# The third expert's rows turned before the second expert's joins, their twelve sums on GpSimd, and its weight sums issued in two parts around a pair's scatters

## The chip, the cores and the metric

The kernel runs on one core of a Trainium2 chip. TensorE (PE) multiplies matrices, VectorE (DVE) and ScalarE (ACT) do elementwise work and read the results out of PSUM, GpSimd (POOL) does elementwise work on SBUF and issues the scatters, and SyncE (SP) issues the loads. Each engine works through its own queue in the order in which the program was written, and waits where an instruction needs something that another engine or a transfer has not finished. The metric is the device time of one execution in microseconds, as the median of several runs.

## The reference, cut to what matters

A linear attention with a per-channel decay makes 3072 rows of 384 numbers. Each row then goes to one of eight experts, chosen by its largest logit, and back to its own place:

```python
logits = x @ w_gate
expert_idx = np.argmax(logits, axis=1)
...
x_sorted = x[perm]
...
h = np.maximum(x_sorted[lo:hi] @ w1[e], 0.0)
y_sorted[lo:hi] = h @ w2[e]
...
y = y_sorted[inv_perm]
return (gate_w[:, None] * y).astype(np.float32)
```

`w1[e]` is 384 x 1024 and `w2[e]` is 1024 x 384. The change lies in this second half.

## The kernel before, in words

The first half of the program is the attention. It scatters each finished row into a table `xs` in device memory, sorted by expert, with a region for each expert. The second half takes the experts one by one, here counted from 0 as in the code. An expert has up to three tiles of 128 rows (`t` = 0, 1, 2). For experts 0 and 1 the first tile is done early, inside the attention, so these two have two tiles left. What does not fit in three tiles goes to "quads" of small pieces.

One expert passes through these steps:

- `load_expert` (line 500) reads its rows from `xs` into `xrow`, with four loads, and their row numbers and gates into `tg`. `load_pads` (line 515) has to write padding behind the expert's rows first. `load_first_weights` and `load_second_weights` load `w1t` and `w2t`. All of them stand in SP's queue.
- `turn` (line 385) transposes the rows on VectorE (`xT`), and casts the row numbers to `dst`, on ScalarE where it is called from `tasks`.
- The product with `w1` of experts 1 to 7 uses a scheme of 20 block products instead of 24, which needs sums of blocks of the weights (`WEIGHT_SUMS`, 16 steps and 17 instructions, since one step takes two; `prepare_weights`, on GpSimd) and twelve sums of blocks of the rows (`ROW_SUMS`; `sum_rows`, on VectorE, or on GpSimd where a task says `add`).
- `widen_sums` (line 1330) runs the 20 products through five PSUM banks (`hps`), in the order of `WIDE_STEPS`. ScalarE copies some results out (`keep`), VectorE joins results with `join`, which reads PSUM, and `more`, which reads SBUF only, and ScalarE applies the relu (`rect`). The first seven copies come before the first join, and the first join comes after the eighth product. The first result of the ninth weight step, `a11`, is read by the tenth product.
- A third tile goes through `narrow_late`. The first two tiles go through `narrow_pair` (line 1403), the product with `w2`, again with sums: in it VectorE joins two halves of each finished tile in `ysb` (line 1434), and GpSimd scatters the tile to the output (line 253). `ysb` has three buffers, used in turn.

`wide_part` and `pair_part` string these together. The table `TASKS` says which work on other experts' rows stands between the steps of expert `e`: hook 0 at the start of `wide_part`, hook 1 after it, hook 2 inside the pair and hook 3 behind it. A task acts on expert `e + 1`, or on `e + 2` with `>` in front. The order of the work is therefore written out by hand, and each engine's queue follows from it.

The early tiles leave with `narrow_early`, whose two scatters carry no group, so the second waits until the first has landed. The other scatters to the output are in the group "out" and don't wait for each other.

For expert 2 the row sums lie in `rooms[1]`, a buffer of the quads' weights that is free by then (the trace calls it `qw`), and expert 1's hidden values lie in `rooms[2]`, also `qw` in the trace.

Of the kernel before, what the change touches and what calls it, by code (L numbers as in the profile page):

```python
# [62 lines left out]


TASKS = {
    0: ("turn sum12", "", "", ">sum2"),
    1: ("", "turn add6", "sum2", "sum2"),
    2: ("turn", "quad0 sum1", "sum7", "sum4"),
    3: ("turn", "sum6", "sum6", ""),
    4: ("sq00 sq01", "turn sum2", "sum7", "sum3"),  # L70
    5: ("sq02 quad1", "sq03 turn", "sum9", "sum3"),
# [10 lines left out]
PLAIN = (0,)  # L82


GT, AHEAD = 2, 5
WEIGHT_SUMS = """
    as0=a30-a32 a32=a12+a32 as1=a32-a30 as2=a30+a31 as3=a10+a11 as4=as3-a01 a31=a21+a31
    a30=-a30-a31 a11=a01-a11 a11=as1-a11 as5=a02+a22 as6=a20-as5 as7=a00-as4 as5=a30-as5
# [74 lines left out]
def _bc(ap, axis, n):  # L163
    shape = list(ap.shape)
    shape.insert(axis, n)
    return ap[tuple([slice(None)] * axis + [None])].to_broadcast(shape)
# [3 lines left out]
def kernel(  # L170
# [15 lines left out]
    nc = tc.nc  # L186
# [40 lines left out]
    def load_gate():  # L227
# [12 lines left out]
        out=ident,  # L240
# [113 lines left out]
    def load_rows(row, count=C):  # L354

        rows = xs[ds(row, count)] if not isinstance(row, int) else xs[row : row + count]
        n, whole = -(-count // C), count // C
        wholes = rowp.tile([128, TILES * C // BK, DB], F32, name="xrow")
        x = wholes[:, 0 : count // BK]
        tg = rowp.tile([128, TILES, USED - TOK], F32, name="tg", bufs=4)[:, 0:n]  # L360
        reads = load_blocks(x, rows)
        reads.append(
            nc.sync.dma_start(
                tg[:, 0:whole], rows[0 : whole * C, TOK:USED].rearrange("(t p) r -> p t r", p=C)
            ).ins
        )
        if n > whole:
            nc.sync.dma_start(tg[0 : count - whole * C, whole], rows[whole * C :, TOK:USED])
        return {"n": n, "rows": count, "x": x, "tg": tg, "reads": reads, "whole": wholes}
# [61 lines left out]
    def narrow(x, t, w, yp, group="out", order=range(NF), late=None):  # L431
        for f in order:
            nc.tensor.matmul(
                yp,
                lhsT=x["hT"][:, f, t * C : t * C + C],
                rhs=w[1][:, f, :],
                start=f == order[0],
                stop=f == order[-1],
            )
        put(x, t, yp, group, late)  # L440

    def put(x, t, yp, group, late=None):
        ysb = ep.tile([128, DM], F32, name="ysb", bufs=3)
        if x.get("wide") or late is not None:
            nc.scalar.mul(ysb, yp, x["tg"][:, t, 1:2])
        else:
            nc.vector.tensor_scalar(ysb, yp, x["tg"][:, t, 1:2], None, op0=OP.mult)
        leave = lambda: scatter(out, x["dst"][:, t : t + 1], ysb, N - 1, group)
        if late is None:
            leave()  # L450
        else:
            late.append(leave)
# [21 lines left out]
    weights = {}  # L474
# [10 lines left out]
    def load_first_weights(e):  # L485
        w1t = wpool.tile([128, KD, F], F32, name="w1t")
        nc.sync.dma_start(w1t, moe_w1[e].rearrange(W1, p=128))
        weights[e] = [w1t]

    def load_second_weights(e):  # L490
        w2t = wpool.tile([128, NF, DM], F32, name="w2t")
        nc.sync.dma_start(w2t, moe_w2[e].rearrange(W2, p=128))
        weights[e].append(w2t)

    def slot(k, s, most):
        return nc.values_load(
            sloti[0:1, k, s : s + 1], [mybir.EngineType.SP], min_val=0, max_val=most
        )

    def load_expert(e):  # L500

        t = int(e < EARLY)
        x = load_rows(first[e] + t * C, int(FIXED[e]) - t * C)
        if e in RIDE:
            rows = xs[ds(slot(0, RIDE[e], NONE), T)]
            nc.sync.dma_start(x["tg"][C - T :, TILES - 1], rows[:, TOK:USED])
        return x
# [7 lines left out]
    def load_pads(e):  # L515

        end = nc.values_load(
            endi[0:1, e : e + 1],
            [mybir.EngineType.SP],
            min_val=first[e],  # L520
            max_val=first[e] + N,
        )
        ins = nc.sync.dma_start(
            xs[ds(end, TILES * C)].rearrange("(t p) r -> p t r", p=C), _bc(pad, 1, TILES)
        ).ins
        tc.declare_no_dep(ins, group="xs", reason="no row is written twice")
        tc.add_to_no_dep_group("xs", ins)
# [31 lines left out]
    with ExitStack() as st:  # L559
# [300 lines left out]
            x["wide"] = False  # L860

        def narrow_early(x, w, yp, late):
            narrow(x, 0, w, yp, None, late=late)

        def settled(n, rt):

# [277 lines left out]
        over = share()  # L1144
        sums()
        rows_of = {}
        for e in range(4):
            load_pads(e)
            if e < 2:
                rows_of[e] = load_expert(e)  # L1150
# [3 lines left out]
        yp = yt[1].rearrange("p h c -> p (h c)")[:, 0:DM]  # L1154
# [18 lines left out]
    with ExitStack() as st:  # L1173
# [94 lines left out]
        def sums_of(table, at, on):  # L1268

            def one(to, a, b, c, d):  # L1270
                summed(on, at(to), (a or "+", at(b)), (c, at(d)))

            return [
                lambda m=m: one(*m)
                for m in re.findall(r"(\w+)=(-?)(\w+)([+-])(\w+)", table)
            ]
# [29 lines left out]

            return at

        def prepare_weights(x, w):
            x["wa"] = weights_at(w)  # L1310
            for step in sums_of(WEIGHT_SUMS, x["wa"], nc.gpsimd):
                step()

        def prepare_rows(x, held=None):
            x["xa"] = rows_at(x, held)
# [4 lines left out]
        def sum_rows(x, count, other=False):  # L1320
            for name, *step in x["todo"][:count]:
                step[other]()
            x["todo"] = x["todo"][count:]
# [177 lines left out]
        def tasks(e, hook):  # L1501
            for ahead, what, n in re.findall(r"(>?)([a-z]+)(\d*)", TASKS[e][hook]):
                if what in ("turn", "sum", "add"):
                    to = rows_of[e + 1 + len(ahead)]
                    if what == "turn":
                        turn(to, by="scalar")
                        prepare_rows(to, rooms[1] if to is rows_of.get(2) else None)
                    else:
                        sum_rows(to, int(n), what == "add")
                elif what == "quad":  # L1510
                    turn(quads[int(n)], qp)
                else:
                    q, g = int(n[0]), int(n[1])
                    turn_quad(quads[q], slice(g, g + 1))
# [6 lines left out]
        def load_first(e):  # L1521
            if e < E:
                rows_of[e] = load_expert(e)
                load_first_weights(e)
# [26 lines left out]
        for leave in waits:  # L1551
            leave()
        s0 = hidden_sums(rows_of[0], nc.gpsimd)
        load_first(2)
        load_pads(4)
        load_pads(5)
        wide_part(1)
        tasks(1, 1)
        prepare_weights(rows_of[2], weights[2])
        load_first(3)  # L1560
        load_pads(6)
        load_pads(7)
# [1 line left out]
        pair_part(  # L1564
            0, s0, lambda: held.append(hidden_sums(rows_of[1], s1=rooms[2][:, 0:HB, 2 * C :]))
        )
        load_second_weights(2)
        fetch(4)
        pair_part(1, held[0])
# [3 lines left out]
        for e in range(2, E):  # L1573
            x, w = rows_of[e], weights[e]
# [24 lines left out]
    with tc.If(todo > 0):  # L1599
# [80 lines left out]
        with ExitStack() as st:  # L1680
            bank, narrow_late, psz = tile_pools(st)
            hp = st.enter_context(tc.tile_pool(name="hp", bufs=1))
            with tc.For_i(0, E) as e:
# [10 lines left out]
                with tc.For_i(e * REGION + skip, rows_to, C) as at:  # L1694
                    x = load_rows(at)
# [57 lines left out]
```

## Time and profile before

| | us |
|---|---|
| median of 3 runs (lowest to highest) | 379.94 (379.58 to 380.77) |
| the profiled execution's own time | 376.19 |
| its span, first to last instruction | 374.3 |
| TensorE busy | 356.7 (95%) |
| VectorE busy | 280.4 (75%) |
| GpSimd busy | 244.8 (65%) |
| ScalarE busy | 172.1 (46%) |
| mean DMA rate | 253 GB/s |

Times inside the trace count from the first instruction. The attention lasts to about 140 us, expert 0's widening (with the plain scheme) from 140 to 151, expert 1's from 151 to 160, the two pairs of these experts from 160 to 179, expert 2's widening from 179 to 203, and the rest of the experts follow at about 30 us each. A timeline row gives start, length, engine, line, operation and operands, then in brackets the idle time of the engine just before it and what ended it. Neighbouring instructions of one kind are merged, with their number as "x4". A TensorE row counts two matmuls for each one of the program. A wait for several things is put down to the one that came last.

### The profile page before, as it was taken

To read this page: it belongs to the slowest core of one execution; us is meant where nothing else is said; L and a number is where in the kernel's file an instruction comes from. 1 tells how busy PE (TensorE), PEld (TensorE's weight loads), DVE (VectorE), ACT (ScalarE), POOL (GpSimd) and SP (SyncE) were. 2 spreads that over 40 slices of the span, in tenths; PEclk is the share of its full clock that TensorE was granted. 3 is DMA by queue.
4 is the path that set the end of the run, shared out by engine and by line. 5 is a ranking of instruction groups with operands and counts; after the bars stand their busy time and mean duration, and the time that the engine had idled before them with its cause. 6 is when DMAs were issued, how large, how long until landed. Compare 5 with 4: busy or idle time off the path is not lost.

```text
span 374.3 us, 9303 instructions
## 1 busy us (share of the span) xinstructions
PE 356.7 (95%) x3470; PEld 310.2 (83%) x3470; DVE 280.4 (75%) x570; ACT 172.1 (46%) x359; POOL 244.8 (65%) x267
## 2 busy tenths in 40 slices
PE   8999999999999999999829999999999999999993
PEld 8889898988989958989728979879699499499692
DVE  6999989897975875398058956967897985878850
ACT  7999785876443202531314335235335235325410
POOL 6344356748964696349869989859939939947103
PEclk9999999999999999999958999999999999999999
DMA  7999765768994437999954369973799989991051
GB/s 253 395 379 381 250 243 200 256 176 285 391 395 158 176 109 220 273 308 339 387 193 101 133 227 389 245 247 102 239 303 367 284 306 381 373 364 48 12 183 66
DMA packets 56773, 94.86 MB, mean 253 GB/s; under 512 B 20952, under 2 KB 40859, under 8 KB 55696
## 3 DMA queue, kind: packets, MB, share of 16 engines
q1 hardware_dynamic: 53552, 84.55, 68.2%
q0 software_dynamic: 3168, 9.64, 6.8%
q8 instruction: 29, 0.48, 0.5%
q14 instruction: 24, 0.20, 0.2%
HBM read 79.16 MB, written 15.21 MB: 252 GB/s over the span
## 4 chain that ended last, share of the span: by engine, by line
PE 43%; POOL 28%; DMA 12%; issue 10%; SPq 3%; DVE 2%; ACT 1%; POOLq 0%; DVEq 0%; ACTq 0%
PE yps L1416 8%; POOL wsum L1257 7%; POOL was L1266 7%; POOL w1t L1266 6%; PE yps L1238 4%; PE s L683 4%; PE hps L1358 4%; POOL out_dram L253 4%; PE yt L707 4%; PE xp L806 3%; DMA xrow<-xs 3%; DMA xs<-xr,posi 3%; PE s L413 3%; PE hps L413 3%; PE kp L696 2%
## 5 line engine op out<-in xcount | busy, mean ns | idle before, releaser
L253 POOL DMA_INDIRECT out_dram<-ysb,dst x26 | 27.3, 1049 | 55.8 <-DVE ysb L1434 33.9
L1376 ACT ACTIVATE hT<-hT 128x352 f32<-128x352 f32 (+1 forms) x48 | 23.9, 506 | 49.4 <-DVE hT L1346 49.2
L1416 PEld LDWEIGHTS yps<-w2t,hT 128*128 128x128 f32 x224 | 36.4, 190 | 4.5 <-issue 2.5
L649 POOL TENSOR_TENSOR k<-k,r 128x1024 f32<-128x1024 f32 (+1 forms) x11 | 25.1, 2284 | 23.0 <-ACT r L645 17.1
L1416 PE MATMUL yps<-w2t,hT 128*128 128x192 f32 x224 | 39.4, 329 | 0.6 <-ACT held L1430 0.5
L1358 PE MATMUL hps<-xbs,w1t 128*128 128x176 f32 (+2 forms) x216 | 36.0, 310 | 0.1
L253 POOL DMA_INDIRECT xs<-xr,posi x24 | 25.6, 1069 | 13.4 <-issue 4.6
L689 DVE COPY_PREDICATED at<-mpack,s 128x512 f32<-128x512 uint8 x48 | 31.9, 728 | 3.0 <-PE s L683 3.0
L1346 DVE TENSOR_TENSOR hT<-hps,hT 128x352 f32<-128x352 f32 (+1 forms) x42 | 22.2, 528 | 15.4 <-PE hps L1358 9.7
L1358 PEld LDWEIGHTS hps<-xbs,w1t 128*128 128x128 f32 x216 | 32.5, 190 | 0.7 <-issue 0.6
L1369 ACT COPY hT<-hps 128x352 f32<-128x352 f32 (+1 forms) x54 | 24.8, 460 | 17.3 <-PE hps L1358 13.8
L1430 ACT ACTIVATE held<-yps,tg 128x192 f32<-128x192 f32 x32 | 13.0, 421 | 37.9 <-DVE ysb L1434 23.9
L1266 POOL TENSOR_TENSOR was<-w1t 128x256 f32<-128x256 f32 x35 | 29.8, 866 | 0.5
L631 DVE TENSOR_TENSOR_SCAN sum<-g,cap 128x1032 f32<-128x1032 f32 (+1 forms) x14 | 28.1, 2012 | 2.2 <-ACT g L624 2.2
L1434 DVE SCALAR_TENSOR_TENSOR ysb<-yps,tg,held 128x192 f32<-128x192 f32 x32 | 12.5, 413 | 20.1 <-DMA out_dram<-ysb,dst 12.4
L1238 PE MATMUL yps<-qw,hqT 128*32 128x192 f32 (+1 forms) x192 | 26.8, 380 | 0.0
L683 PE MATMUL s<-q,k 64*128 64x128 f32 x384 | 26.3, 281 | 0.2
L1266 POOL TENSOR_TENSOR w1t<-w1t 128x256 f32<-128x256 f32 x28 | 24.9, 889 | 1.6 <-PE yt L1134 1.1
L683 PEld LDWEIGHTS s<-q,k 64*128 64x128 f32 x384 | 22.8, 187 | 2.7 <-issue 0.9
L806 PE MATMUL xp<-wx,ys 128*128 128x104 f32 x192 | 24.9, 279 | 0.2 <-ACT ys L770 0.2
L707 PE MATMUL yt<-at,v 128*48 128x128 f32 x384 | 24.3, 276 | 0.0
L806 PEld LDWEIGHTS xp<-wx,ys 128*128 128x128 f32 x192 | 22.9, 192 | 1.0 <-ACT ys L770 0.3
(191 smaller groups left out, 884.6 us busy)
## 6 DMA issues: line engine op xcount, KB each, us to landing
w1t<-in_moe_w_dram SPq DMA_DIRECT2D x8, 1536.0 KB, 8.9
w2t<-in_moe_w_dram SPq DMA_DIRECT2D x8, 1536.0 KB, 14.1
qw<-in_moe_w_dram SPq DMA_DIRECT2D x16, 768.0 KB, 10.9
qw<-in_moe_w_dram SPq DMA_DIRECT2D x8, 1536.0 KB, 16.3
k<-in_ku_dram SPq DMA_DIRECT2D x12, 512.0 KB, 6.9
q<-in_qu_dram SPq DMA_DIRECT2D x12, 512.0 KB, 6.0
f<-in_fu_dram SPq DMA_DIRECT2D x10, 512.0 KB, 5.8
xs<-pad SPq DMA_DIRECT2D x8, 600.0 KB, 8.2
```

Source lines behind the costliest of these rows:

```text
L253: ins = nc.gpsimd.indirect_dma_start(out=dst, out_offset=bass.IndirectOffsetOnAxis(ap=idx, axis=0), in_=src, in_offset=None, bounds_check= ...
L631: nc.vector.tensor_tensor_scan(x["sum"][:, part].rearrange("p s c -> p (s c)"), x["g"][:, part].rearrange("p s c -> p (s c)"), cap[:, part ...
L649: ins = on.tensor_tensor(k, k, units[u]["r"][:, part], op=OP.mult).ins
L683: done["score"] = nc.tensor.matmul(ps[h][:, p], lhsT=x["k"][r, s], rhs=x["q"][r, s], start=True, stop=True).ins
L689: nc.vector.copy_predicated(x["at"][:, a, h], _bc(causal, 1, HP), x["ps", a][h])
L707: nc.tensor.matmul(x["yt"][a][DP * (h ^ a) : DP * (h ^ a) + D, p], lhsT=x["v"][:, a, 2 * p + h], rhs=x["at"][:, a, h, p], start=p == 0, st ...
L806: nc.tensor.matmul(x["xp", a][:, p], lhsT=x["ys", a][:, p], rhs=wx[:, p, 0:XW] if a else wx[:, p, E:WX], start=True, stop=True,)
L1238: nc.tensor.matmul(yp[r], lhsT=h[:, f, at : at + T], rhs=w[:, f, cols], start=f == order[0], stop=f == order[-1], skip_group_check=True,)
L1257: on.tensor_tensor(to, a, b, op=OP.subtract)
L1266: on.tensor_tensor(to, first[1], second[1], op=op)
L1358: nc.tensor.matmul(banks[n][:, g], lhsT=lhs[:, C * g : C * g + C], rhs=rhs, start=op == "new" and g == 0, stop=True, skip_group_check=True,)
L1416: nc.tensor.matmul(to, lhsT=h[:, f], rhs=w[:, f], start=start and f == 0, stop=f == HB - 1, skip_group_check=True,)
```

## The change

Expert 2's rows are turned at the start of expert 1's `wide_part` and not behind it. All twelve sums of its rows are on GpSimd, where six were before and six were spread over VectorE's queue. Its 17 weight instructions come in two parts: eight steps (nine instructions) ahead of the first pair, and the other eight behind it. The turn of expert 3's rows is written at the end of pair 1 and not at the start of expert 2's widening; its place in VectorE's queue stays. Expert 2's rows are loaded ahead of the pads of expert 3, and the two early scatters join the group "out".

```diff
 TASKS = {
-    0: ("turn sum12", "", "", ">sum2"),
-    1: ("", "turn add6", "sum2", "sum2"),
-    2: ("turn", "quad0 sum1", "sum7", "sum4"),
+    0: ("turn sum12", "", "", ""),
+    1: ("turn add12", "", "", ">turn"),
+    2: ("", "quad0 sum1", "sum7", "sum4"),
...
-GT, AHEAD = 2, 5
+GT, AHEAD, HALFWAY = 2, 5, 8
...
-            narrow(x, 0, w, yp, None, late=late)
+            narrow(x, 0, w, yp, "out", late=late)
...
-        for e in range(4):
+        for e in range(3):
             load_pads(e)
...
-        def prepare_weights(x, w):
+        def prepare_weights(x, w, count=None):
             x["wa"] = weights_at(w)
-            for step in sums_of(WEIGHT_SUMS, x["wa"], nc.gpsimd):
+            x["left"] = sums_of(WEIGHT_SUMS, x["wa"], nc.gpsimd)
+            sum_weights(x, len(x["left"]) if count is None else count)
+
+        def sum_weights(x, count):
+            for step in x["left"][:count]:
                 step()
+            x["left"] = x["left"][count:]
...
         s0 = hidden_sums(rows_of[0], nc.gpsimd)
-        load_first(2)
+        rows_of[2] = load_expert(2)
+        load_pads(3)
+        load_first_weights(2)
         load_pads(4)
         load_pads(5)
         wide_part(1)
-        tasks(1, 1)
-        prepare_weights(rows_of[2], weights[2])
+        prepare_weights(rows_of[2], weights[2], HALFWAY)
...
         pair_part(
             0, s0, lambda: held.append(hidden_sums(rows_of[1], s1=rooms[2][:, 0:HB, 2 * C :]))
         )
+        sum_weights(rows_of[2], len(rows_of[2]["left"]))
```

GpSimd's queue from expert 0's hidden sums (`hT`) to pair 0's scatters, before. The rows `qw<-` are the sums of expert 2's rows, `w1t` and `was` are its weight sums, and the scatters write `out_dram`:

```order
L1257 TENSOR_TENSOR hT<-hT 128x4x128
L1266 TENSOR_TENSOR qw_2121<-xT 128x192 x2
L1266 TENSOR_TENSOR qw_2121<-xT,qw_2121 128x192 x2
L1266 TENSOR_TENSOR qw_2121<-qw_2121,xT 128x192
L1266 TENSOR_TENSOR qw_2121<-xT 128x192
L1266 TENSOR_TENSOR was_2361<-w1t 128x256
...
L1263 TENSOR_TENSOR w1t<-w1t 128x256
L1266 TENSOR_TENSOR w1t<-w1t 128x256
...
L1266 TENSOR_TENSOR w1t<-w1t,was_2379 128x256
L253 DMA out_dram<-ysb,dst 3072x384 x4
```

And after:

```order
L1257 TENSOR_TENSOR hT<-hT 128x4x128
L1266 TENSOR_TENSOR qw_2110<-xT 128x192 x2
L1266 TENSOR_TENSOR qw_2110<-xT,qw_2110 128x192 x2
L1266 TENSOR_TENSOR qw_2110<-qw_2110,xT 128x192
...
L1266 TENSOR_TENSOR qw_2110<-xT,qw_2110 128x192 x4
L1266 TENSOR_TENSOR was_2367<-w1t 128x256
...
L1263 TENSOR_TENSOR w1t<-w1t 128x256
L253 DMA out_dram<-ysb,dst 3072x384 x2
L1266 TENSOR_TENSOR w1t<-w1t 128x256
...
L1266 TENSOR_TENSOR w1t<-w1t,was_2471 128x256
L253 DMA out_dram<-ysb,dst 3072x384 x2
```

The sums of rows are twelve and not six, the weight sums are parted behind L1263, and pair 0's two scatters stand in the gap. Pair 1's two stay behind the second part.

VectorE's queue at expert 1's joins (L1346, `qw_2122` being its hidden values), before, from its last row sum (`xbs`) to the first join, and from the last join to pair 0's sums:

```order
L1266 TENSOR_TENSOR xbs_2163<-xT,xbs_2151 128x128
L1346 TENSOR_TENSOR qw_2122<-hps,qw_2122 128x2x128
...
L1346 TENSOR_TENSOR qw_2122<-qw_2122,hold 128x2x128
L393 STREAM_TRANSPOSE xT<-xrow 128x12x3x32
L1257 TENSOR_TENSOR hT<-hsum,hT 128x4x128
```

And after, where the joins are L1351:

```order
L1266 TENSOR_TENSOR xbs_2152<-xT,xbs_2140 128x128
L393 STREAM_TRANSPOSE xT<-xrow 128x12x3x32
L1351 TENSOR_TENSOR qw_2111<-hps,qw_2111 128x2x128
...
L1351 TENSOR_TENSOR qw_2111<-qw_2111,hold 128x2x128
L1257 TENSOR_TENSOR hT<-hsum,hT 128x4x128
```

The transpose of expert 2's rows moved from behind sixteen joins to ahead of them. Six row sums further down in this queue are gone.

ScalarE's queue at the start of expert 1's widening, before, from expert 0's last relu (L427) on (L1369 copies results out of PSUM):

```order
L427 ACTIVATE hT<-hps 128x2x256 x4
L1369 COPY qw_2122<-hps 128x2x128 x7
L1376 ACTIVATE qw_2122<-qw_2122 128x2x128
L1369 COPY hold<-hps 128x2x128
L1369 COPY qw_2122<-hps 128x2x128
```

And after:

```order
L427 ACTIVATE hT<-hps 128x2x256 x4
L400 CAST dst<-tg 128x3
L1374 COPY qw_2111<-hps 128x2x128 x7
L1381 ACTIVATE qw_2111<-qw_2111 128x2x128
L1374 COPY hold<-hps 128x2x128
```

The cast of expert 2's row numbers, which reads `tg`, stands now ahead of the seven copies. Before it stood behind all of expert 1's relus.

## The prediction

> **What bounds the kernel now.** I read the page's slices first, then busy time in short windows, then each engine's timeline around the place where they break. Experts count from 0 as in the code: the third expert, whose rows are moved, is expert 2, and a "pair" is `narrow_pair` of one expert.
>
> ```profile
> PE   8999999999999999999829999999999999999993
> PEclk9999999999999999999958999999999999999999
> ```
>
> TensorE (PE) is full in nearly every slice. The one dip away from the ends is slices 20 and 21 of 40 (9.36 us each), where the granted clock drops too.
>
> ```profile
> 186.00:188.00 2.00, 0.00 (x0) 0.00 (x0) 0.00 (x0) 0.00 (x0) 1.70 (x2) 1.00 1.05 371
> 188.00:190.00 2.00, 0.00 (x0) 0.00 (x0) 0.00 (x0) 0.00 (x0) 0.14 (x1) 0.56 1.07 381
> ...
> 198.00:200.00 2.00, 2.00 (x12) 2.00 (x12) 1.97 (x4) 0.89 (x2) 1.92 (x3) 0.88 0.36 77
> ```
>
> Columns: length, busy PE, weight load, VectorE (DVE), ScalarE (ACT), GpSimd (POOL), clock, DMA share, GB/s. From 186 to 190 nothing computes except two scatters on GpSimd, and the clock is at 0.56 after 188; it is back at 0.88 only in 198 to 200.
>
> ```profile
> 178.85 0.81 PE L1358 MATMUL hps<-xT,was 128*128 128x192 f32 x4
> ...
> 183.40 2.11 PE L1358 MATMUL hps<-qw,w1t 128*128 128x192 f32 x12
> 194.05 2.93 PE L1358 MATMUL hps<-qw,was 128*128 128x192 f32 x8 [8.54 <-DVE hT L1346]
> ...
> 198.93 2.11 PE L1358 MATMUL hps<-qw,w1t 128*128 128x192 f32 x12
> ```
>
> TensorE did ten products of expert 2's widening, had no PSUM bank for the eleventh, and idled 8.54 us for VectorE's first join.
>
> ```profile
> 177.82 0.42 DVE L1434 SCALAR_TENSOR_TENSOR ysb<-yps,tg,held 128x192 f32<-128x192 f32 x1 [0.65 <-PE yps L1416]
> 190.65 0.74 DVE L1434 SCALAR_TENSOR_TENSOR ysb<-yps,tg,held 128x192 f32<-128x192 f32 x2 [12.41 <-DMA out_dram<-ysb,dst]
> 191.30 0.62 DVE L1266 TENSOR_TENSOR qw<-xT,qw 128x192 f32<-128x192 f32 x2
> 191.84 1.72 DVE L393 STREAM_TRANSPOSE xT<-xrow 128x1152 f32<-128x1152 f32 x1
> 193.47 0.53 DVE L1346 TENSOR_TENSOR hT<-hps,hT 128x384 f32<-128x384 f32 x1
> ```
>
> VectorE waited 12.41 us for a scatter. `ysb` has three buffers; early tiles took 0 and 1, pair 0 took 2 and 0, pair 1 takes 1 and 2, so pair 1's second tile needs pair 0's first scatter landed. Behind that wait stood two row sums, a transpose, and the join TensorE needed.
>
> ```profile
> 164.39 1.97 POOL L1266 TENSOR_TENSOR qw<-xT 128x192 f32<-128x192 f32 x2 [10.05 <-DVE xT L393]
> 166.43 2.20 POOL L1266 TENSOR_TENSOR qw<-xT,qw 128x192 f32<-128x192 f32 x2
> ...
> 169.59 0.60 POOL L1266 TENSOR_TENSOR qw<-xT 128x192 f32<-128x192 f32 x1
> 170.15 0.72 POOL L1266 TENSOR_TENSOR was<-w1t 128x256 f32<-128x256 f32 x1
> ...
> 174.84 1.32 POOL L1266 TENSOR_TENSOR was<-was,w1t 128x256 f32<-128x256 f32 x1
> ...
> 178.65 0.73 POOL L1266 TENSOR_TENSOR w1t<-w1t 128x256 f32<-128x256 f32 x1
> ...
> 184.56 1.04 POOL L253 DMA_INDIRECT out_dram<-ysb,dst  x1 [0.16 <-issue]
> 185.90 0.97 POOL L253 DMA_INDIRECT out_dram<-ysb,dst  x1 [0.30 <-issue]
> ```
>
> That scatter was late only by its place in the queue: GpSimd idled 10.05 us for expert 2's transpose, then did six row sums (164.39 to 170.15, 5.76 us) and seventeen weight instructions before it.
>
> **The change: what it takes away.** (1) The idle of 8.54 us. (2) The cold clock behind it. The same four groups of products are in expert 3:
>
> ```profile
> 226.50 1.46 PE L1358 MATMUL hps<-xbs,was 128*128 128x192 f32 x8
> ...
> 229.09 2.11 PE L1358 MATMUL hps<-xbs,w1t 128*128 128x192 f32 x12
> ```
>
> They take 229.09 − 226.50 = 2.59 us there and 198.93 − 194.05 = 4.88 us behind the stall: 2.29 us more. Together 10.83 us can go.
>
> On the clock, the Trainium skill ("TensorE: Matmul & The Clock Gate", "What's actually happening") says that one idle window of about 3.4 us halves the clock and one busy window of that length restores it. The windows agree in kind. An estimate from the page's figure, 3.4 us at half rate, costs 1.7 us where the rows show 2.29, and the gain below would be 0.6 us smaller.
>
> **Does the wait really go?** Expert 2's transpose now stands ahead of expert 1's joins, when its rows have landed.
>
> ```profile
> 147.27 1.99 SPq L347 DMA_DIRECT2D xrow<-xs  x4
> 149.36 0.42 SPq L363 DMA_DIRECT2D tg<-xs  x1
> ...
> xrow<-xs SPq DMA_DIRECT2D x1, 144.0 KB, 3.8
> tg<-xs SPq DMA_DIRECT2D x1, 3.0 KB, 3.5
> ```
>
> The fourth row load starts near 148.8 and lands 3.8 us later, at 152.6; with pad 3 moved behind these loads, no later. The transpose lasts 1.7 us and ends near 154.4, inside an idle stretch of VectorE, whose first join came at 154.54:
>
> ```profile
> 154.54 0.42 DVE L1346 TENSOR_TENSOR qw<-hps,qw 128x256 f32<-128x256 f32 x1 [5.95 <-PE hps L1358]
> ...
> 162.55 1.75 DVE L393 STREAM_TRANSPOSE xT<-xrow 128x1152 f32<-128x1152 f32 x1
> ```
>
> GpSimd then starts at 154.5 in place of 164.39. Twelve sums at the measured rate (5.76/6 = 0.96 us) take 11.5, to 166.0; the first nine weight instructions 8.5 (170.15 to 178.65), to 174.5; so the scatter goes at about 174.7 and frees its buffer 6.1 us later (184.56 to 190.65): 180.8. Pair 1's joins want it at about 180.5 (TensorE left pair 1 at 179.0, and terms 3 and 4 below add 1.5), so 0.3 us of wait remain. Joins and transpose need what they needed from 190.65 to 193.47, less the two row sums (0.62): 2.2 us. The first join is possible at 183.0; TensorE runs out of banks at 185.51 (183.40 + 2.11) plus the delay below, 187.0. There are 4 us of cover, so the exact rate of GpSimd is worth nothing until it is 4 us worse. Both ends of that rate are in the second rival.
>
> The second part of the weight sums moves behind two scatters: 174.7 + 2.7 (twice 184.56 to 185.90) = 177.4, and 5.9 more (178.65 to 184.56) to 183.3. Its first result is read by the tenth product, near 186, the last by the eighteenth; hidden. The six sums taken from VectorE cost it nothing that TensorE waited for except the 0.62 counted above. The early scatters' dependency removed lets GpSimd go on sooner, but its next work waits for expert 0's relu on ScalarE: nothing gained. Pad 3 on SP behind the rows: its bytes only move towards `w1t`, first read by GpSimd at 166 rather than 170; I take nothing, and up to 1 us is inside the cover.
>
> **What it adds.** (3) On ScalarE the cast of `dst` now stands ahead of the seven copies that free banks for expert 1's products, and waits for `tg`.
>
> ```profile
> 150.90 0.60 ACT L427 ACTIVATE hT<-hps 128x512 f32<-128x512 f32 x1 [1.99 <-PE hps L413]
> 151.40 3.00 ACT L1369 COPY qw<-hps 128x256 f32<-128x256 f32 x7
> ```
>
> `tg` landed at 149.36 + 3.5 = 152.9, so the copies start up to 1.6 us later than 151.40; without pad 3 ahead perhaps 0.3 us later. Part can hide in banks that are still free. Behind the waiting cast stand all of ScalarE's copies, and TensorE and VectorE wait for those, so what doesn't hide is paid in full. Between 0 and 1.6 I take 0.9.
>
> (4) GpSimd now works during expert 1's joins, which ran alone before. What that costs shows in the same operation elsewhere:
>
> ```profile
> L1346 DVE TENSOR_TENSOR hT<-hT 128x384 f32<-128x384 f32 x4 | 4.2, 1059 | 0.2
> L1346 DVE TENSOR_TENSOR hT<-hps,hT 128x384 f32<-128x384 f32 x7 | 3.8, 546 | 1.0 <-ACT hT L1369 0.9
> ...
> L1346 DVE TENSOR_TENSOR hT<-hT 128x384 f32<-128x384 f32 x4 | 2.5, 628 | 0.2
> ```
>
> The first two rows are expert 2's joins, the third expert 3's, all beside GpSimd. Joins that read PSUM keep 546 ns; the SBUF-to-SBUF ones range from 628 to 1059, a spread of 0.43. Expert 1 has six of these, three before the bank of the last new product is free (by `WIDE_STEPS`). Three times 0.2 (nearer to 628) is 0.6 us; the ends are 0 and 1.3. The transpose (1.75) that left the far side of these joins pays for what follows.
>
> The Trainium skill speaks against this part ("GPSIMD Engine Reference", "8. Key points"): GpSimd shares its SBUF interfaces with VectorE and contends with instructions that have two SBUF inputs. The rows agree: only such joins are stretched. If each of the three waited out the whole spread, this term would be 1.3 and the gain 0.7 us smaller.
>
> **Sum.** 8.54 + 2.29 − 0.9 − 0.6 = 9.3 us. The profiled execution lasted 376.19 us around a span of 374.3, so its span should come to 365.0; the median of the runs is 379.94, 3.75 above that execution, and I take the difference from the median: **370.6 us**. After the stall everything shifts: the slices of TensorE show nothing but nines from there to the last one, and most loads start when the same work frees their buffers.
>
> **The rivals.** *Loads do not shift along.* SP's queue between 180 and 203 waits for transfers, not for the stall:
>
> ```profile
> 203.05 0.76 SPq L487 DMA_DIRECT2D w1t<-in_moe_w_dram  x1
> ...
> w1t<-in_moe_w_dram SPq DMA_DIRECT2D x8, 1536.0 KB, 8.9
> ```
>
> Expert 4's `w1t` still starts at 203 and lands about 212.7; GpSimd read it at 225.54, now about 216, so 3 us of cover remain; the quad's rows, issued just before, have less. If these are 3 us short, 373.6. I give 8%.
>
> *GpSimd still late.* Twelve sums at 1.12 us (dearest pair of the six) and nine weight instructions at 1.3 (dearest of them) end at 179.8; scatter landed 186.1, first join 188.4, done 189.0: TensorE idles 2.0 us, 372.6. At 0.6 a sum (the cheapest) nothing changes, for the bound is then elsewhere. 12%.
>
> *The rows land late.* Transpose and cast stand at the head of both queues, and nothing behind them can pass. Expert 3's `tg` and the slowest of the quad's row loads needed
>
> ```profile
> tg<-xs SPq DMA_DIRECT2D x1, 3.0 KB, 7.1
> ...
> qrow<-xs SPq DMA_DIRECT2D x1, 12.0 KB, 12.7
> ```
>
> With 7.1 us `tg` lands at 156.5, 5.1 after 151.40; that idle also brings the cold clock (2.3): 8.0 with term 4, leaving 2.8, so 377.1. 8%. *On the other side*, the same block with the quad's 12.7 us: 162.1, a wait of 10.7 + 2.3 + 0.6 = 13.6, 2.8 us slower than before, 382.7. It decides from 7.9 us of wait, a landing at 159.3. Against both: the 1.5 MB loads that the slow ones queued behind are issued after these rows. 4%.
>
> *The change misses its wait*: pair 1 is held by another scatter of the several it waits on, and TensorE by the same 8.5 us: 379.9. The others in its list stand in GpSimd's queue ahead of the sums at 164.39, over 13 us before the wait, so 4%.
>
> **How the numbers follow.** Forecast 64%, with a range of its own from 369.1 (terms 3 and 4 free) to 372.0 (both at their dear end). With 12% at 372.6, 8% at 373.6, 8% at 377.1, 4% at 379.9 and 4% at 382.7, a range up to 375.0 leaves 16% out above; downward 0.5 us more for the measurement, 368.6. A change under 0.3% cannot be told from none here. Faster by more: 64 + 12 + 8 + 8 = 92%; same 4%; slower 4%.
>
> **What would show it.** The wait of 12.41 us before L1434 under 2 us; no idle of TensorE over 1 us between 150 and 300; clock 1.00 in every window there; pair 0's scatters on GpSimd near 175; copies of expert 1 starting 0.3 to 1.6 us later; the later stages unchanged in length. Wrong would be: a `dst` cast or transpose that waits several microseconds near 152, or a new wait for `qrow` or `w1t` near 200 to 216.

## The result, and the profile after

| | before | after |
|---|---|---|
| median of 6 runs each, taken side by side (lowest to highest), us | 379.61 (379.10 to 380.77) | 370.81 (370.18 to 371.74) |
| ratio, with its 95% interval | | 0.9767 (0.9747 to 0.9787) |
| the profiled execution's own time, us | 376.19 | 370.18 |
| its span, us | 374.3 | 368.4 |
| mean granted clock of TensorE (1 is full speed) | 0.984 | 0.996 |

The change saved 8.8 us, with 370.6 forecast and 370.81 measured. The two spans differ by only 5.9 us, because the attention of the two profiled executions differed although the program is the same there. The first product of expert 0's widening, in TensorE's timeline of the kernel before:

```profile
140.34 10.52 PE L413 MATMUL hps<-xT,w1t 128*128 128x256 f32 x48
```

and of the kernel after:

```profile
143.08 10.52 PE L413 MATMUL hps<-xT,w1t 128*128 128x256 f32 x48
```

From that row on, before took 374.3 − 140.34 = 233.96 us and after 368.4 − 143.08 = 225.32, which is 8.64 less and agrees with the medians. All comparisons below are of stages, each from the start of its first product to the start of the next stage's; times inside a trace are compared relative to that row.

| stage, us | before | after | difference | forecast |
|---|---|---|---|---|
| expert 0's widening | 10.36 | 10.36 | 0.00 | 0 |
| expert 1's widening | 9.04 | 10.32 | +1.28 | +1.5 |
| the pairs of experts 0 and 1 | 19.11 | 19.18 | +0.07 | 0 |
| expert 2's widening | 23.97 | 13.56 | −10.41 | −10.83 |
| the rest | 171.48 | 171.90 | +0.42 | 0 |

The slices of TensorE and of its clock, from the page of the kernel after:

```profile
PE   8999999999999899999999999999999999999992
PEclk9999999999999999999999999999999999999998
```

The hole of slices 20 and 21 is gone, in busy time and in clock. TensorE's timeline where it idled for 8.54 us before:

```profile
187.49 2.11 PE L1363 MATMUL hps<-qw,w1t 128*128 128x192 f32 x12
189.44 1.46 PE L1363 MATMUL hps<-qw,was 128*128 128x192 f32 x8
```

The eleventh and twelfth products follow without idle, and take 1.46 us where they took 2.93. VectorE's timeline at the place where it waited:

```profile
183.14 0.74 DVE L1439 SCALAR_TENSOR_TENSOR ysb<-yps,tg,held 128x192 f32<-128x192 f32 x2 [0.81 <-PE yps L1421]
183.80 1.77 DVE L393 STREAM_TRANSPOSE xT<-xrow 128x1152 f32<-128x1152 f32 x1
188.41 0.56 DVE L1351 TENSOR_TENSOR hT<-hps,hT 128x384 f32<-128x384 f32 x1 [2.84 <-PE hps L1363]
189.07 1.36 DVE L1351 TENSOR_TENSOR hT<-hT 128x384 f32<-128x384 f32 x1
```

The wait of 12.41 us for a scatter is now 0.81 us for TensorE. VectorE was ready for the first join at 183.80 + 1.77 = 185.57 and waited 2.84 us for the product: it is ahead of TensorE where it was behind. GpSimd's timeline after:

```profile
157.41 1.15 POOL L1266 TENSOR_TENSOR qw<-xT 128x192 f32<-128x192 f32 x2 [0.46 <-DVE xT L393]
...
162.65 2.42 POOL L1266 TENSOR_TENSOR qw<-xT,qw 128x192 f32<-128x192 f32 x4
165.03 0.72 POOL L1266 TENSOR_TENSOR was<-w1t 128x256 f32<-128x256 f32 x1
...
174.20 1.04 POOL L253 DMA_INDIRECT out_dram<-ysb,dst  x1 [0.15 <-issue]
...
186.30 1.83 POOL L1257 TENSOR_TENSOR wsum<-w2t 128x768 f32<-128x768 f32 x1
188.21 3.90 POOL L1257 TENSOR_TENSOR wsum<-w2t,wsum 128x768 f32<-128x768 f32 x2
```

The twelve sums took 165.03 − 157.41 = 7.62 us, 0.635 each, not 0.96. The first scatter went 31.1 us after the start of expert 0's widening, where the kernel before had 184.56 − 140.34 = 44.2. The new cost is on ScalarE:

```profile
155.69 0.19 ACT L400 CAST dst<-tg 128x3 int32<-128x3 f32 x1 [1.45 <-DMA tg<-xs]
155.79 2.45 ACT L1374 COPY qw<-hps 128x256 f32<-128x256 f32 x7
```

and, in TensorE's timeline, the idle that follows from it:

```profile
156.25 0.68 PE L1363 MATMUL hps<-xbs,was 128*128 128x128 f32 x4 [0.87 <-POOL hsum L1478]
```

The copies started 151.40 − 140.34 = 11.06 us after expert 0's widening before, and 12.71 after: 1.65 later. The bracket on TensorE's row names a GpSimd sum; the bank it needed is freed by the copies, which the runs below confirm.

### The profile page after: what moved, and what is told of

Read it like the earlier page. It is cut to its first block, busy times and chain, and to the rows that moved or that the text cites. A ratio compares the mean times of both kernels' runs of the same rounds, so it can differ in the third digit from the quotient of the medians.

```text
span 368.4 us, 9304 instructions
## 1 busy us (share of the span) xinstructions
PE 355.9 (97%) x3470; PEld 308.8 (84%) x3470; DVE 277.6 (75%) x564; ACT 172.2 (47%) x359; POOL 249.0 (68%) x273
## 4 chain that ended last, share of the span: by engine, by line
PE 58%; POOL 20%; issue 8%; DMA 5%; DVE 5%; ACT 1%; SPq 1%; POOLq 0%; DVEq 0%
PE yps L1421 11%; PE hps L1363 8%; PE s L683 6%; PE xp L806 6%; PE yt L707 6%; POOL wsum L1257 6%; POOL was L1266 5%; POOL w1t L1266 5%; PE yps L1238 5%; POOL out_dram L253 3%; PE yt L728 3%; PE dp L744 3%; PE kp L696 2%; DMA v<-in_vu_dram 2%; PE s L413 2%
## 5 line engine op out<-in xcount | busy, mean ns | idle before, releaser
L1381 ACT ACTIVATE hT<-hT 128x352 f32<-128x352 f32 (+1 forms) x48 | 23.9, 506 | 38.6 <-DVE hT L1351 38.4
L253 POOL DMA_INDIRECT xs<-xr,posi x24 | 27.5, 1144 | 15.8 <-issue 4.6
L1351 DVE TENSOR_TENSOR hT<-hps,hT 128x352 f32<-128x352 f32 (+1 forms) x42 | 22.2, 529 | 18.2 <-PE hps L1363 12.5
L631 DVE TENSOR_TENSOR_SCAN sum<-g,cap 128x1032 f32<-128x1032 f32 (+1 forms) x14 | 29.2, 2095 | 1.9 <-ACT g L624 1.8
L1257 POOL TENSOR_TENSOR wsum<-w2t,wsum 128x768 f32<-128x768 f32 x12 | 22.5, 1873 | 0.9
```

What stands on the lines that cost most here:

```text
L253: ins = nc.gpsimd.indirect_dma_start(out=dst, out_offset=bass.IndirectOffsetOnAxis(ap=idx, axis=0), in_=src, in_offset=None, bounds_check= ...
L631: nc.vector.tensor_tensor_scan(x["sum"][:, part].rearrange("p s c -> p (s c)"), x["g"][:, part].rearrange("p s c -> p (s c)"), cap[:, part ...
L1257: on.tensor_tensor(to, a, b, op=OP.subtract)
```

## The experiments

The runs came in three companies, that is, groups of runs taken together (e1 to e4, e5 to e8, e9 to e12), and each had its own runs of the kernel before: a median of 380.79 us in the first, 375.47 in the second, 375.59 in the third. So each run is given as a difference from, and a ratio to, the kernel before of its own company.

| run | us | less than before by | ratio (95% interval) |
|---|---|---|---|
| e1 weight sums parted, nothing else | 376.07 | 4.72 | 0.9892 (0.9855 to 0.9929) |
| e2 turn early, nothing else | 371.33 | 9.46 | 0.9750 (0.9709 to 0.9791) |
| e3 changed, weight sums not parted | 373.58 | 7.21 | 0.9827 (0.9789 to 0.9865) |
| e4 before, own buffer for pair 1's second tile | 373.21 | 7.58 | 0.9812 (0.9777 to 0.9847) |
| e5 the changed kernel | 367.48 | 7.99 | 0.9789 (0.9765 to 0.9813) |
| e6 changed, cast behind | 367.25 | 8.22 | 0.9786 (0.9755 to 0.9817) |
| e7 turn early, parted, six sums on VectorE | 366.62 | 8.85 | 0.9767 (0.9744 to 0.9790) |
| e8 e3 with own buffer | 366.65 | 8.82 | 0.9764 (0.9744 to 0.9785) |
| e9 e7 with cast behind | 365.10 | 10.49 | 0.9740 (0.9716 to 0.9764) |
| e10 the changed kernel | 366.32 | 9.27 | 0.9764 (0.9744 to 0.9784) |
| e11 loads and group alone | 375.23 | 0.36 | 0.9994 (0.9978 to 1.0010) |
| e12 the kernel before, profiled again | 376.15 | | one run |

Differences under some 1 us between rows of different companies say nothing: the changed kernel itself stands at 8.80, 7.99 and 9.27.

**Is it the wait for the buffer?** e4 moves nothing. It gives pair 1's second tile memory of its own, so that this tile needs no scatter landed:

```diff
-            ysb = [ep.tile([128, DM], F32, name="ysb", bufs=3) for t in range(2)]
+            own = x is rows_of[1]
+            ysb = [ep.tile([128, DM], F32, name="ysb", bufs=3) for t in range(1 if own else 2)]
+            if own:
+                ysb.append(rooms[1].rearrange("p f d -> p (f d)")[:, 6 * DM : 7 * DM])
```

> The kernel before, nothing moved, but the second tile of pair 1 goes to a piece of memory of its own and not to the third ysb buffer. Theory A: VectorE no longer waits for pair 0's scatter although that still goes at 184.6; TensorE's 8.54 us and the cold clock go, and nothing is paid in expert 1's widening: 368.5 to 370 us. Rival D (the late weight sums or late scatters on GpSimd hold TensorE themselves, the buffer is only the first to show it): 374 us or more.

The wait is confirmed and the total is not. Expert 2's widening took 13.00 us (23.97 before) and expert 1's 9.03, without cost; that is 11 us. But the whole came out only 7.58 us faster. GpSimd was as late as before, and its lateness came back in expert 3: its `wsum` sums for that expert started 7.1 us into that expert's widening, where in the changed kernel they started 0.2 us before it. TensorE's timeline of this run:

```profile
221.92 0.89 PE L1358 MATMUL hps<-xbs,was 128*128 128x192 f32 x4 [1.64 <-ACT hold L1369]
...
225.44 0.89 PE L1358 MATMUL hps<-xbs,w1t 128*128 128x192 f32 x4 [1.33 <-POOL was L1266]
...
240.57 2.76 PE L1419 MATMUL yps<-wsum,hT 128*128 128x192 f32 x8 [1.93 <-DVE hT L1257]
```

VectorE's, at the same place:

```profile
218.11 2.74 DVE L1346 TENSOR_TENSOR hT<-hT 128x384 f32<-128x384 f32 x1
...
225.33 0.56 DVE L1346 TENSOR_TENSOR hT<-hT 128x384 f32<-128x384 f32 x1
```

and GpSimd's:

```profile
218.61 1.82 POOL L1257 TENSOR_TENSOR wsum<-w2t 128x768 f32<-128x768 f32 x1
220.51 3.90 POOL L1257 TENSOR_TENSOR wsum<-w2t,wsum 128x768 f32<-128x768 f32 x2
```

The same join, SBUF to SBUF, takes 0.56 us at 225.33 and 2.74 at 218.11, beside GpSimd's `wsum` sums; the banks come free later, and TensorE waits 1.64 and 1.33 us. The third wait, of 1.93 us, is not for a bank but for VectorE's sum of hidden values (L1257), which stood behind six sums of expert 4's rows that ran beside GpSimd's weight sums. This profile is of the slowest of the five runs (375.81; the others 373.13 to 373.66, at mean clocks of 0.996 to 0.999 where this one had 0.991), so not all of this need be in the others.

**Which part of the change brings the gain?** e2 changes one line of the table, so that the turn stands ahead of expert 1's joins; e1 parts the weight sums and does nothing else.

```diff
-    1: ("", "turn add6", "sum2", "sum2"),
+    1: ("turn", "add6", "sum2", "sum2"),
```

> The kernel before with only expert 2's turn moved to the start of expert 1's widening; six sums stay on GpSimd, six on VectorE, all 17 weight instructions stay ahead of pair 0's scatters, pads as before. Theory A: GpSimd's sums start about 9 us earlier, the scatter goes near 175 and the wait is gone: 370.3 to 372 us, nearly the whole change. Rival B2 (the twelve sums on GpSimd and the parting are needed as well): 374 us or more.

```diff
-        prepare_weights(rows_of[2], weights[2])
+        prepare_weights(rows_of[2], weights[2], HALFWAY)
...
+        sum_weights(rows_of[2], len(rows_of[2]["left"]))
         load_second_weights(2)
```

> The kernel before with only the weight sums of expert 2 in two parts (nine instructions ahead of pair 0, eight behind it); turn, row sums and loads as before. Theory A (VectorE's wait is for pair 0's first scatter to land, and only its place in GpSimd's queue sets that): the scatter goes at 178.8 in place of 184.56 and lands at 184.9, the first join of expert 2 is at about 187.8, TensorE idles 2 to 3 us in place of 8.54, and 5.7 us of idle plus 0 to 2.3 us of cold clock are gained: 371.6 to 373.9 us. Rival B (the early turn is what the gain comes from, the parting only tidies): 378.5 to 380.5 us.

The early turn alone is worth as much as the whole change. Its VectorE timeline shows a wait that remains and costs nothing:

```profile
185.53 0.74 DVE L1434 SCALAR_TENSOR_TENSOR ysb<-yps,tg,held 128x192 f32<-128x192 f32 x2 [2.84 <-DMA out_dram<-ysb,dst]
...
188.78 0.56 DVE L1346 TENSOR_TENSOR hT<-hps,hT 128x384 f32<-128x384 f32 x1 [0.25 <-PE hps L1358]
```

VectorE still waited 2.84 us for the scatter and then 0.25 us for TensorE: it had caught up before TensorE was out of banks. Parting alone fell between its two expectations: 4.72 us faster. It brings the scatter 5.7 us forward (38.5 us after the start of expert 0's widening, 44.2 before), and VectorE's wait falls to 7.08 us. But the two row sums and the transpose still stood between that wait and the first join, as VectorE's timeline shows:

```profile
188.98 1.30 DVE L1266 TENSOR_TENSOR qw<-xT,qw 128x192 f32<-128x192 f32 x2
190.21 1.69 DVE L393 STREAM_TRANSPOSE xT<-xrow 128x1152 f32<-128x1152 f32 x1
```

TensorE's timeline of e1:

```profile
192.40 2.59 PE L1363 MATMUL hps<-qw,was 128*128 128x192 f32 x8 [3.87 <-DVE hT L1351]
...
199.37 0.89 PE L1363 MATMUL hps<-qw,w1t 128*128 128x192 f32 x4 [1.13 <-POOL was L1266]
```

Of the idle of 8.54 us, 3.87 are left, and it is long enough to cool the clock; another idle of 1.13 us comes later, as in e3 below. This run's windows (columns as in the prediction):

```profile
192.00:194.00 2.00, 1.60 (x6) 1.60 (x7) 1.90 (x2) 0.00 (x0) 2.00 (x2) 0.70 1.04 365
194.00:196.00 2.00, 2.00 (x8) 1.94 (x7) 1.24 (x2) 1.19 (x3) 1.92 (x2) 0.50 0.34 127
```

e11 makes the remaining edits alone, the order of the loads and the group of the early scatters:

```diff
-            narrow(x, 0, w, yp, None, late=late)
+            narrow(x, 0, w, yp, "out", late=late)
...
-        for e in range(4):
+        for e in range(3):
...
-        load_first(2)
+        rows_of[2] = load_expert(2)
+        load_pads(3)
+        load_first_weights(2)
```

> The kernel before with only the order of the loads (expert 2's rows ahead of expert 3's pads) and the early scatters in the group out. Theory A (they carry nothing by themselves): within 0.3% of the kernel before, ratio 0.997 to 1.003, VectorE's wait of some 12 us and TensorE's idle of 8.5 us unchanged. Rival (they let GpSimd or the rows go on sooner and carry a part of the gain): 0.5 to 1.5 us faster, with pair 0's first scatter earlier than 44 us after the start of expert 0's widening.

They carry nothing, as the ratio says, and TensorE's row reads as before:

```profile
193.69 2.93 PE L1358 MATMUL hps<-qw,was 128*128 128x192 f32 x8 [8.54 <-DVE hT L1346]
```

**How much cover is there, and what lies behind it?** e3 is the changed kernel with all seventeen weight instructions ahead of the scatters; e8 is e3 with the buffer of e4.

```diff
-        prepare_weights(rows_of[2], weights[2], HALFWAY)
+        prepare_weights(rows_of[2], weights[2])
```

> The changed kernel with all 17 weight instructions ahead of pair 0's scatters. Theory A: GpSimd ends them near 180.2 by the clock of the changed kernel's profile, the scatter lands at about 186.5, VectorE waits 3.4 us for it, its first join is at 189.0 where the eleventh product wants a bank at 189.4: 370.8 to 371.4 us, the parting is worth under 0.6 us. Rival C (the parting carries its 5.7 us by itself): 375 us or more.

> The changed kernel with all seventeen weight instructions ahead of pair 0's scatters, as in the run that was 2.8 us slower, and pair 1's second tile in memory of its own, so that no join waits for a scatter. Theory A (late scatters cost through the wait for the buffer alone): the 2.8 us come back, 370.6 to 371.2 where the changed kernel has 370.8. Theory E (GpSimd's lateness also costs by itself, its wsum sums then lie beside expert 2's joins and lengthen those in SBUF): the idle of 0.82 us goes, the one of 1.33 us stays, 372.0 to 373.0.

e3 met neither expectation. Relative to expert 0's widening its scatter went at 38.4 us, 7.3 later than in the changed kernel, which is 4 us later than the prediction's 174.7 − 140.34 = 34.4 and so right at the end of the forecast cover. TensorE's timeline of e3:

```profile
190.52 1.57 PE L1363 MATMUL hps<-qw,was 128*128 128x192 f32 x8 [0.82 <-DVE hT L1351]
...
196.48 0.89 PE L1363 MATMUL hps<-qw,w1t 128*128 128x192 f32 x4 [1.33 <-POOL was L1266]
```

The wait itself cost 0.82 us, about what that cover says. Another 1.33 us came later, and expert 2's widening took 16.11 us, 2.55 more than in the changed kernel. VectorE's timeline:

```profile
187.63 0.74 DVE L1439 SCALAR_TENSOR_TENSOR ysb<-yps,tg,held 128x192 f32<-128x192 f32 x2 [5.20 <-DMA out_dram<-ysb,dst]
...
193.82 2.04 DVE L1351 TENSOR_TENSOR hT<-hT 128x384 f32<-128x384 f32 x1
```

and GpSimd's:

```profile
188.65 0.97 POOL L253 DMA_INDIRECT out_dram<-ysb,dst  x1 [3.40 <-PE hps L1363]
189.62 1.84 POOL L1257 TENSOR_TENSOR wsum<-w2t 128x768 f32<-128x768 f32 x1
191.54 3.91 POOL L1257 TENSOR_TENSOR wsum<-w2t,wsum 128x768 f32<-128x768 f32 x2
```

The lateness goes round in a loop. VectorE waits for a scatter, so it finishes pair 1's second tile late; GpSimd waits 3.40 us to scatter that tile; its `wsum` sums therefore start 6.6 us into expert 2's widening and not 3.4 as in the changed kernel, beside the joins on which the later banks depend. e8 takes the buffer out of this loop and leaves GpSimd's queue as it was: its scatter goes at the same 38.4 us, `wsum` starts 3.5 us into the widening, the widening takes 13.68 us, TensorE's timeline shows no idle in it, and the time is 0.8 us below the changed kernel's in the same company (e5), which is no more than the changed kernel's own gains differ by (7.99 to 9.27). So theory A holds for a scatter as late as this: it costs through the buffer alone, and the stall beside `wsum` was its consequence. For GpSimd as late as in the kernel before it does not hold: in e4, with the scatter at 44.4 us, VectorE waited for no scatter, and expert 3 paid.

**What is the early cast worth?** e6 is the changed kernel with expert 2's `dst` cast behind expert 1's joins; the transpose stays early.

```diff
-    def turn(x, pool=None, by="vector"):
+    def turn(x, pool=None, by="vector", cast=True):
...
-        if "tg" in x:
+        if "tg" in x and cast:
+            number(x, by)
+
+    def number(x, by="vector"):
+        n = x["n"]
+        if True:
             x["dst"] = ep.tile([128, TILES], I32, name="dst", bufs=4)[:, 0:n]
...
-                        turn(to, by="scalar")
+                        turn(to, by="scalar", cast=to is not rows_of.get(2))
...
         wide_part(1)
+        number(rows_of[2], "scalar")
```

> The changed kernel with expert 2's dst cast moved behind expert 1's joins on ScalarE; the transpose stays early. Theory A (the cast that waits for tg holds ScalarE's seven copies): the copies start about 1.6 us earlier, TensorE's idle of 0.87 us in expert 1's widening goes, that widening takes 9.4 us in place of 10.3, and the time is 0.9 us below the changed kernel, 369.6 to 370.2 where that has 370.8. Theory B (GpSimd beside VectorE's joins is what lengthens that widening): it stays at 10.3 us and the time is within 0.3 us of the changed kernel's.

Expert 1's widening took 9.17 us, where e5, the changed kernel in the same company, had 10.12. The copies start earlier and TensorE's idle there is gone, so theory A is right about the mechanism: 0.95 us. The total moved by only 0.2 us, however, and expert 2's widening took 14.19 us where e5 had 13.57. TensorE's timeline of e6:

```profile
189.82 0.89 PE L1368 MATMUL hps<-qw,w1t 128*128 128x192 f32 x4 [0.95 <-POOL was L1271]
```

VectorE's:

```profile
187.15 2.06 DVE L1356 TENSOR_TENSOR hT<-hT 128x384 f32<-128x384 f32 x1
```

and GpSimd's:

```profile
184.88 3.92 POOL L1262 TENSOR_TENSOR wsum<-w2t,wsum 128x768 f32<-128x768 f32 x2
```

TensorE came earlier by the cast and GpSimd did not, so `wsum` fell onto a later join, and 0.62 us of the 0.95 was given back. This run's six times fall in two groups (365.46 to 366.26, and 368.24 to 368.54); the profile is of the lower group, and what the upper one did stays open.

**Do the twelve sums on GpSimd help?** e7 has the early turn and the parted weight sums, with six row sums left on VectorE as before; e9 adds the late cast of e6.

```diff
-    1: ("turn add12", "", "", ">turn"),
+    1: ("turn", "add6", "sum2", "sum2"),
```

(The rest of `TASKS`, the loads and the early scatters as before.)

> The kernel before with the early turn and the parted weight sums, but six of the twelve row sums left on VectorE, and the loads as before. Theory A (once the turn is early, only GpSimd's queue ahead of the scatter counts): pair 0's first scatter goes at about 171 us, VectorE waits for no scatter, 370.5 to 371.1 where the changed kernel has 370.8: the place of the six sums is worth nothing. Theory B (the six sums on VectorE, 0.62 us of them just ahead of the transpose, cost what they take): 371.3 to 372, as with the early turn alone.

> The parted version with six sums left on VectorE, and expert 2's dst cast behind expert 1's joins. Theory A (the cast alone costs some 1.1 us in expert 1's widening, and GpSimd, with six sums less, keeps ahead, so that its wsum sums do not move onto expert 2's joins): expert 1's widening 9.3 us, expert 2's 13.0 to 13.2, the time 1.6 to 2.2 us below the changed kernel's in the same company. Theory B (what the cast brings is given back in expert 2's widening, as in the run with the cast behind and twelve sums on GpSimd): expert 2's widening 13.6 to 14.2 and the time within 1.0 us of the changed kernel's.

e7 is 0.86 us below e5 in the same company, at the edge of what the runs can tell; expert 2's widening took 13.00 us. Moving the other six sums to GpSimd brought nothing. e9's stages fit theory A, its time neither theory: expert 1's widening 9.35 us, expert 2's 13.00, and the time 1.22 us below the changed kernel in the same company; four of its five runs (364.85 to 365.54, the fifth 367.13) lie under all five of the changed kernel's (365.82 to 367.48). The forecast was 1.6 to 2.2. VectorE's timeline shows one place where the rest went:

```profile
199.72 0.71 DVE L393 STREAM_TRANSPOSE qxT<-qrow 128x384 f32<-128x384 f32 x1 [1.76 <-DMA qrow<-xs]
```

The quad's rows did not arrive earlier with the rest. Expert 2's narrow steps, up to expert 3's first product, took 18.03 us in e9 and 17.07 in the changed kernel beside it (e10). The changed kernel can meet the same wait: in e5 these steps took 18.21 us, and VectorE's timeline of e5 has

```profile
201.97 0.70 DVE L393 STREAM_TRANSPOSE qxT<-qrow 128x384 f32<-128x384 f32 x1 [1.37 <-DMA qrow<-xs]
```

Of the twelve experiments, e9 has the largest gain over the kernel before.

**The yardsticks.** The changed kernel twice, and the kernel before with a second profile:

> The changed kernel once more, on the chip of the next three, as their yardstick. All theories: a ratio to the kernel before of 0.9767, between 0.9747 and 0.9787 (about 371 us), with expert 1's widening at 10.3 us and expert 2's at 13.6.

> The changed kernel, as the yardstick of the one before it: 0.977 to 0.979 of the kernel before.

> The kernel before, unchanged, for a second profile of it: expert 0's widening starts near 140 or near 143 us, whichever the changed kernel has beside it; from there on the stages are those of the first profile within 0.3 us: expert 1's widening 9.0 us, the pairs 19.1, expert 2's widening 24.0, the rest 171.5.

e12's stages are 9.04, 19.11, 24.20 and 170.79 us, those of the first profile but for 0.7 us in the rest; the changed kernel's in e5 and e10 are 10.12 and 10.25, 19.19 and 19.18, 13.57 and 13.56, 172.63 and 170.46. So the stages around the change repeat within 0.3 us and the long rest within 2.2.

## Why the prediction was right

*The wait for pair 0's scatter is what held expert 2.* Shown three ways: by an earlier scatter (e2), by a buffer that needs no scatter (e4), and by putting the scatter part of the way back (e3, and e8 with the buffer). The path came as forecast: the transpose of expert 2's rows ended 157.33 − 143.08 = 14.25 us after the start of expert 0's widening, where 154.4 − 140.34 = 14.1 was expected, the granted clock was 1.00 in every 2 us window from 146 to 300 us, and TensorE's longest idle in that stretch was 0.87 us.

*Idle and cold clock, 10.83 us.* Measured 10.41, and 10.4 to 10.6 in the other profiles of the changed kernel. The missing 0.4 lies with a stretched join (the row of 1.36 us above) beside `wsum`, as far as the runs can be compared: with six sums on GpSimd `wsum` started 2.6 us into the widening in place of 3.4, and that stage took 13.00 us, all of the 10.83 and a little more. That the clock cools by itself behind an idle was seen again in e1: 3.87 us of idle, and the same eight products took 2.59 us as against 1.46.

*The cast ahead of the seven copies, 0.9 us.* Its size is 0.95 (e6 against e5) and 1.03 (e9 against e7): right. The copies came 1.65 us later, 0.05 beyond the range given.

*GpSimd beside expert 1's joins, 0.6 us.* Mis-sized: with the cast out of the way, expert 1's widening took 9.17 and 9.35 us against 9.04 before, so 0.1 to 0.3. The step that failed is taking the stretch from expert 2's joins. Those ran beside other GpSimd work, and the sums of 128x192 hardly disturb. VectorE's timeline of the profile after, three of expert 1's six SBUF joins:

```profile
158.91 0.61 DVE L1351 TENSOR_TENSOR qw<-qw 128x256 f32<-128x256 f32 x1
161.00 0.43 DVE L1351 TENSOR_TENSOR qw<-qw 128x256 f32<-128x256 f32 x1
...
165.18 0.86 DVE L1351 TENSOR_TENSOR qw<-qw,hold 128x256 f32<-128x256 f32 x1
```

All six took 0.42 to 0.43 us before. The last two (0.86 and 0.97) are stretched, but they lie beside the weight sums, from 165.03 on, and behind expert 1's last product, where the pairs show little of it (+0.07). The Trainium skill ("GPSIMD Engine Reference", "8. Key points") names contention for such joins, and that section gives no size; here the stretch ran from nothing to 2.2 us (0.56 alone, 2.74 in e4), and the long cases lay beside `wsum`, whose instructions take 1.8 to 2.0 us each.

*GpSimd's twelve sums at 0.96 us.* Mis-sized in the safe direction: 0.635. The rate was read from sums most of which ran beside VectorE's own SBUF work; that this is the reason was not tested. The first scatter went 31.1 us after the start of expert 0's widening, where 34.4 was expected. As the prediction said, it made no difference.

*Four microseconds of cover.* The point was about right (e3 stood there and lost 0.82 us to the wait). That GpSimd's rate is "worth nothing until it is 4 us worse" is shown near the forecast only (e2's scatter went 34.6 us after the start of expert 0's widening, and TensorE had no idle for it); no run stood between that and e3. The price behind the point was too low: the second rival counted the wait alone, and 1.33 us more came with `wsum`.

*Loads.* "After the stall everything shifts" failed for the loads just behind it, and the condition of the rival that loads don't shift along came true. SP's timeline after:

```profile
206.17 0.36 SPq L487 DMA_DIRECT2D w1t<-in_moe_w_dram  x1
```

Expert 4's `w1t` was issued 63.1 us after the start of expert 0's widening, and 62.7 before, although TensorE was 9 us further on. The cover that the rival counted was enough in the first profile and in e10; in e5 the same kernel had the wait for the quad's rows and took 1.1 us longer there, and in e9, which is some 2 us further on, it came too. The rest of the program moved by +0.42 us, within what it varies from one profile of the same kernel to the next.

So the mechanism was right, and that 9.3 us came so close to the 8.8 measured is in part luck: the stall was taken 0.4 us too large and the added terms 0.2 too large (1.5 against 1.28), which partly cancel, and the 0.07 and 0.42 us of the other stages were not forecast and lie within what the stages vary by. What the prediction didn't see is that the early turn is enough: beside it, parting the weight sums only pays for the six sums added to GpSimd (e2 has neither and e3 the six sums without the parting; in the same company e3 was 2.25 us slower).

## What to carry to other kernels

When an engine waits for a buffer, look at what stands in the freeing engine's queue ahead of the release; here one transpose written earlier in one queue let another engine start 10 us earlier, and that alone was the gain. After removing such a wait, look at what the lateness of the off-path engine still collides with: e4 removed the same wait and gave part of the gain back in the next expert, where GpSimd's sums then lay beside VectorE's joins and row sums. An operation that moves ahead takes its small companions with it: a cast of 0.19 us, which waited for its load at the head of ScalarE's queue, cost 1 us, and could stay behind.

## What was not expected of the hardware

A short idle can cool TensorE's clock. In the profiled execution of e4 the idle of 1.93 us before 240.57 was followed by eight products in 2.76 us in place of 1.46, at these granted clocks (windows of that run):

```profile
240.00:242.00 2.00, 1.43 (x5) 1.46 (x6) 1.90 (x4) 0.42 (x2) 1.33 (x1) 0.68 0.07 25
242.00:244.00 2.00, 2.00 (x8) 2.00 (x7) 1.92 (x7) 0.73 (x3) 0.00 (x0) 0.50 0.19 73
```

After e3's idle of 1.33 us the granted clock stayed at 1.00. One execution shows the cooling; the other four of e4 have a mean clock of 0.996 to 0.999, so either this idle or its effect was missing there, and the exact threshold stays open. The Trainium skill ("TensorE: Matmul & The Clock Gate", "What's actually happening") gives about 3.4 us of idle for this; this trace shows it after 1.93 us.

How long expert 2's widening takes follows where GpSimd's `wsum` sums fall: starting 2.6 us into it 13.00 us (e7, e9), 3.4 us 13.56 (the changed kernel), 3.5 us 13.68 (e8), 4.4 us 13.95 (e2), 4.7 us 14.19 (e6), 6.6 us 16.11 (e3, with 0.82 of it the wait), and 11.1 us, behind its last critical join, 13.00 again (e4). That order is read off these runs; no run moved `wsum` alone.

The attention, which no edit touches, ended 142.95 to 143.63 us into the span in all profiles of the first company and 139.29 to 140.90 in all of the second and third. It explains most of the 5 us between the medians of the kernel before; its cause was not looked for further and stays open.
